# Weight decoding in 40 units of 512 columns instead of 80 of 256, in buffers and banks of its own

## The chip, the cores and the metric

The kernel runs on one core of a Trainium2 chip. The core has five engines that run side by side, each through its own list of instructions in order: TensorE (PE, matrix multiplication; its weight loads are listed apart as PEld), VectorE (DVE), ScalarE (ACT), GpSimd (POOL) and SyncE (SP, which issues all transfers here). Engines wait for each other through semaphores. SBUF is the working memory of 128 partitions; PSUM is the memory into which TensorE writes, eight banks of 512 fp32 columns in each partition. The metric is the time of one execution on the device in microseconds (us), the median of several runs. Less is better.

## The reference

An attention that keeps, for each query, the 32 largest of 576 scores, and behind it a chain of linear layers:

```python
batch, n_heads, seq, head_dim = 8, 8, 576, 64
scores = 1.0 / np.sqrt(64) * np.matmul(q, k.transpose(0, 1, 3, 2))
kth = np.partition(scores, -32, axis=-1)[..., -32:-31]
scores = np.where(scores >= kth, scores, -1e9)
attn = softmax(scores)                      # by max, exp, sum
x = (attn @ v) as [4608 tokens, 512]
a, b = x @ w1, x @ w2                       # w1, w2: 512 x 1024
h = (a * b) @ w3                            # w3: 1024 x 1024
out = h @ w_out                             # w_out: 1024 x 512
```

The four weights come as float64. The chip has no float64, so the kernel turns each number into an fp32 by itself ("decoding"); `w3 @ w_out` is folded into one matrix `wf` before it is used, and `w1`, `w2` and `wf` are each kept as a high and a low part.

## The kernel before

**Slots and periods.** The attention is cut into 144 slots (8 batches, each 18: four pairs of heads by four query tiles of 128, and two ends). A loop over `p` (L504) works on several slots at once in each round, called a period here: scores of slot p+1 (`st` on PE, copied to `s` by ACT), the search for the 32 largest of slot p (`w` and `top` on DVE), masking and exponent of slot p-1 (`pab`: ACT, POOL, ACT), and transposition (`tp`, `ro`), values (`ro`) and normalising (`pr`, `x`) of slot p-2. A period begins here with DVE's two maxima and minima of the score thirds (`w<-s`, L212-213). Twelve slots make a block of 384 tokens; when its `x` is complete (first at p = 14), its linear layers (`moe_steps`) are queued, and `fill` issues 24 of their 288 matrix multiplications in each period (`SHARE`, L44). After the last period the rest is issued.

**Order.** Each engine keeps the order in which the program is written (`InOrder`, L47). Where an instruction waits, all behind it on its engine wait too.

**Decoding.** At six places in each period the loop calls `warm()` (L487). Before, each call starts one new unit of 256 columns and takes every unit under way one step further. A unit (`decode`, L107): ACT writes the scaled high words to the PSUM tile `t` and the scaled low words to `r`, step 1; DVE takes sign and shifted bits of `t` into `u`, two instructions, step 2; POOL adds `u` and `r` as integers, step 3; one step of rest. Then:
- `w_out` (16 units): the sum is written to `wo`, done.
- `w3` (32 units, four for each of eight pieces `f`): at step 5 two matrix multiplications of the unit with `wo` into the PSUM tile `pf` (fp32; the trace shows each as two passes); after the fourth unit ACT copies `pf` to the high part of `wf`, DVE takes the rest as the low part.
- `w1`, `w2` (32 units): at step 5 ACT casts to `wh`, at step 6 POOL subtracts for `wl`.

The list `startup` (L159) runs through `w_out`, then by turns four units of `w3` and two of `w1`, then `w2`: 80 units at six a period, thus until p = 13. I call periods 3 to 10 the fold periods (8 matrix multiplications into `pf` in each), 11 to 13 the `w2` periods.

**Buffers.** The raw bits `z` of a unit lie in the pool of the layers' buffers `g` (8 buffers, L101); `t` (two units to a bank), `pf` and the layers' PSUM tiles share three banks in turn (`ps_m`). `prefetch` asks for transfers up to four units ahead on SP's queue, which also carries q, k, v and the output. On any of these, a new tile waits until the one that had its place before is done with.

Of the kernel before, what the change touches and what calls it, by code (L numbers as in the profile page):

```python
# [21 lines left out]
DM, DF = 512, 1024  # L22
NCC, NFC, NEC = DM // 128, DF // 128, DM // 128
# [3 lines left out]
NB = 384  # L27
# [12 lines left out]
STEEP = 2.0**80  # L40
SCALE = 0.125
S_BUFS = 3
WAITING = 4
SHARE = 8, 8, 8  # L44


# [21 lines left out]
def attn_moe(ctx: ExitStack, tc: tile.TileContext, q, k, v, w1, w2, w3, w_out, out, flag, general):  # L68
    nc = tc.nc
    pe, act, dve, pool, sp = nc.tensor, nc.scalar, nc.vector, nc.gpsimd, nc.sync  # L70
# [2 lines left out]
    kv_p = ctx.enter_context(tc.tile_pool(name="kv", bufs=NHP))  # L73
    att_p = ctx.enter_context(tc.tile_pool(name="att", bufs=2))
    small = ctx.enter_context(tc.tile_pool(name="small", bufs=4))
    x_p = ctx.enter_context(tc.tile_pool(name="x", bufs=2 * NHP))
    g_p = ctx.enter_context(tc.tile_pool(name="g", bufs=NFC))
    o_p = ctx.enter_context(tc.tile_pool(name="o", bufs=2))
    ps_a = ctx.enter_context(tc.tile_pool(name="ps_a", bufs=2, space=PSUM))
    ps_v = ctx.enter_context(tc.tile_pool(name="ps_v", bufs=1, space=PSUM))  # L80
    ps_m = ctx.enter_context(tc.tile_pool(name="ps_m", bufs=3, space=PSUM))

    ident = const.tile([128, 128], F32, name="ident")
    make_identity(nc, ident)
# [13 lines left out]
        pe, act, dve, pool, sp = (InOrder(tc, e) for e in (pe, act, dve, pool, sp))  # L98

    def fetch(src):  # L100
        z = g_p.tile([128, 2 * NB], F32, tag="g", name="z")  # L101
        sp.dma_start(z[:, :512].bitcast(I32), src)
        return z

    bank = []

    def decode(z, dst=None):  # L107
        if not bank:
            both = ps_m.tile([128, 512], F32, tag="mm", name="t")
            bank.extend((both[:, 256:], both[:, :256]))  # L110
        t = bank.pop()
        high = z[:, 1:512:2]
        low = z[:, :512].bitcast(U16)[:, 1:1024:4]
        sign, u, r = (z[:, i * 256 : (i + 1) * 256].bitcast(I32) for i in range(3))
        act.activation(t, high, AF.Copy, scale=2.0**-112)
        act.activation(r, low, AF.Copy, scale=2.0**-13)
        yield
        ti = t.bitcast(I32)
        dve.tensor_scalar(sign, ti, -(2**31), None, op0=ALU.bitwise_and)
        dve.scalar_tensor_tensor(u, ti, 3, sign, op0=ALU.logical_shift_left, op1=ALU.bitwise_or)  # L120
        yield
        dst = z[:, :256] if dst is None else dst
        pool.tensor_tensor(dst.bitcast(I32), u, r, op=ALU.add)
        yield
        yield
        return dst

    def load_w12(i, c, z):
        if len(wl) == i:
            wl.append(const.tile([128, NCC * DF], F32R, tag="wl1", name="wl1"))  # L130
        cut = slice(c * 256, (c + 1) * 256)
        y = yield from decode(z)
        act.copy(wh[i][:, cut], y)
        yield
        pool.tensor_tensor(wl[i][:, cut], y, wh[i][:, cut].bitcast(F32), op=ALU.subtract)

    def load_wout(c, z):
        yield from decode(z, wo[:, c * 256 : (c + 1) * 256])

    fold = {}  # L140

    def load_w3(c, z):
        f, i = c // 4, c % 4
        y = yield from decode(z)
        if i == 0:
            fold[f] = ps_m.tile([128, 512], F32, tag="mm", name=f"pf{f}")
        for j in range(2 * i, 2 * i + 2):
            pe.matmul(
                fold[f], y[:, (j % 2) * 128 : (j % 2 + 1) * 128], wo[:, j * DM : (j + 1) * DM],
                start=(j == 0), stop=(j == NFC - 1),  # L150
            )
        if i == 3:
            cut = slice(f * DM, (f + 1) * DM)
            yield
            act.copy(wf[0][:, cut], fold[f])
            yield
            dve.tensor_tensor(wf[1][:, cut], fold[f], wf[0][:, cut].bitcast(F32), op=ALU.subtract)

    startup = [(w_out[c], lambda z, c=c: load_wout(c, z)) for c in range(16)]  # L159
    for f in range(NFC):  # L160
        startup += [(w3[c], lambda z, c=c: load_w3(c, z)) for c in range(4 * f, 4 * f + 4)]
        startup += [(w1[c], lambda z, c=c: load_w12(0, c, z)) for c in range(2 * f, 2 * f + 2)]
    startup += [(w2[c], lambda z, c=c: load_w12(1, c, z)) for c in range(16)]

    def at(x, b, *i):
        return x[(b, *i)] if isinstance(b, int) else x[(ds(b, 1), *i)].rearrange("o p n -> (o p) n")
# [149 lines left out]
    def width(t):  # L316
        return 64 if t == TAIL else 128

    def new_x():
        return x_p.tile([128, 2, NB], F32R, tag="x", name="x")  # L320

    def normalise(ov, rec):
        dve.tensor_tensor(rec, ov, rec, op=ALU.mult)
# [11 lines left out]
    def moe_steps(xs, nb, places, after):  # L335
        def take_a(p, asb):
            act.copy(asb[:, :nb], p[:, :nb])

        def take_b(p, asb, gf):
            whole = asb[:, :nb]  # L340
            dve.tensor_tensor(whole, p[:, :nb], whole, op=ALU.mult)
            act.copy(gf[:, 0, :nb], whole)
            pool.tensor_tensor(gf[:, 1, :nb], whole, gf[:, 0, :nb].bitcast(F32), op=ALU.subtract)

        def take_o(p, e):
            osb = o_p.tile([128, NB], F32, tag="o", name="osb")
            act.copy(osb[:, :nb], p[:, :nb])
            for place, cut in places:
                sp.dma_start(place(slice(e * 128, (e + 1) * 128)), osb[:, cut])

        g = []
        for f in range(NFC):
            asb = o_p.tile([128, NB], F32, tag="o", name="asb")
            g.append(g_p.tile([128, 2, NB], F32R, tag="g", name="g"))
            for i in range(2):
                p = ps_m.tile([128, 512], F32, tag="mm", name="ab")
# [12 lines left out]
                yield  # L369
        for e in range(NEC):  # L370
            p = ps_m.tile([128, 512], F32, tag="mm", name="eo")
            for f in range(NFC):
                for n, (i, j) in enumerate(((0, 0), (1, 0), (0, 1))):
                    pe.matmul(
                        p[:, :nb], wf[i][:, f * DM + e * 128 : f * DM + (e + 1) * 128], g[f][:, j, :nb],
                        start=(f == 0 and n == 0), stop=(f == NFC - 1 and n == 2),
                    )
                    if (f, n) != (NFC - 1, 2):
                        yield
            after(lambda p=p, e=e: take_o(p, e))  # L380
            yield

    if general:
        outs = out.rearrange("e (b t) -> b e t", b=B)
        for src, step in startup:
            for _ in step(fetch(src)):
                pass
        with tc.For_i(0, B, 1) as b:
            seen = small.tile([1, 1], I32, tag="seen", name="seen", bufs=1)
            nc.sync.dma_start(seen, flag[ds(b + 1, 1), :])  # L390
            with tc.If(nc.values_load(seen, min_val=0, max_val=1) > 0):
                kts = {hp: load_k(b, hp) for hp in range(NHP)}
                vts = {hp: load_v(b, hp) for hp in range(NHP)}
                for first, ts in ((0, range(3)), (NB, range(3, TAIL + 1))):
                    xs, lo = [new_x() for _ in range(NHP)], 0
# [64 lines left out]

    def begin():
        while starting:
            n = starting.pop(0)
            queue.append(moe_steps([xs[n, hp] for hp in range(NHP)], NB, places[n], put_off.append))

# [16 lines left out]
    def prefetch(n):  # L482
        while waiting and len(fetched) < n:
            src, step = waiting.pop(0)
            fetched.append((fetch(src), step))

    def warm():  # L487
        if p < 0:
            return
        if fetched:  # L490
            z, step = fetched.pop(0)
            going.append(step(z))
        going[:] = [unit for unit in going if next(unit, "end") != "end"]
        prefetch(WAITING)

# [8 lines left out]
    for p in range(-1, n_slots + 3):  # L504
# [51 lines left out]
        if 0 <= m < n_slots:  # L556
            n = m // BLOCK
            for hp in hps:
                if (n, hp) not in xs:
                    xs[n, hp] = new_x()  # L560
# [16 lines left out]
    wp = ps_m.tile([128, 512], F32, tag="mm", name="wp")  # L577
# [57 lines left out]
```

## Time and profile before

| | |
|---|---|
| median of 3 runs (lowest, highest) | 1321.85 us (1321.67, 1322.46) |
| the profiled execution | 1321.85 us |
| its span in the trace | 1320.0 us |
| PE, DVE, ACT, POOL busy over the span | 94%, 90%, 73%, 65% |
| chain that ended last, by engine | PE 87%, DVE 4%, POOL 3%, ACT 2% |

The shares over the whole span hide that the run has three parts: about 206 us in which weights are decoded beside the attention (periods 0 to 13 and what lies ahead of them), some 1050 us in which layers and attention run together, and a tail with the layers of the last block. The profiled execution's own time is 1.85 us more than its span. The granted clock of TensorE is 1.00 in the middle part, where full is 2.4 GHz; in the first part it falls to half (1.2 GHz) in places, and a window's clock is then between the two.

### The profile page before, as it was taken

How to read it: one execution, taken by the hardware profiler on the slowest of the kernel's cores; microseconds unless marked ns; L12 is line 12 of the kernel's file. 1: busy time of each engine (PE TensorE's matmuls, PEld its weight loads, DVE VectorE, ACT ScalarE, POOL GpSimd, SP SyncE). 2: the span in 40 equal slices, each digit the busy share in tenths (PEclk: the TensorE clock that was granted, in tenths of full speed). 3: DMA queues.
4: the chain of work that ended last, by engine and by line, in shares of the span. 5: the costliest groups of instructions: out<-in, count | busy, mean ns of one | idle time of the engine just before them, and what ended most of it. 6: DMA issues, size and time to landing. Idle time of an engine off the chain costs nothing.

```text
span 1320.0 us, 28196 instructions
## 1 busy us (share of the span) xinstructions
PE 1235.3 (94%) x9617; PEld 1047.7 (79%) x9617; DVE 1194.1 (90%) x4012; ACT 965.9 (73%) x2057; POOL 853.7 (65%) x1225
## 2 busy tenths in 40 slices
PE   2788858999999999999999999999999999999996
PEld 1334436888888888888888888888888888888996
DVE  7988898999999999999999999999999999999610
ACT  5766786877777877777877877778777778777621
POOL 4767697666766766667757757757667666667510
PEclk9899967999999999999999999999999999999998
DMA  6333331200121001100120012110220012000000
GB/s 243 91 101 123 110 96 29 81 22 21 29 74 32 9 27 64 53 27 16 39 84 20 10 33 79 32 33 10 65 60 9 15 47 81 22 21 1 13 13 27
DMA packets 35886, 64.82 MB, mean 49 GB/s; under 512 B 6036, under 2 KB 12180, under 8 KB 35732
## 3 DMA queue, kind: packets, MB, share of 16 engines
q1 hardware_dynamic: 35732, 62.93, 15.3%
q8 instruction: 77, 1.26, 0.4%
q14 instruction: 77, 0.63, 0.2%
HBM read 53.48 MB, written 9.44 MB: 48 GB/s over the span
## 4 chain that ended last, share of the span: by engine, by line
PE 87%; DVE 4%; POOL 3%; ACT 2%; issue 2%; DMA 1%; SPq 0%; POOLq 0%
PE ab L57 32%; PE eo L57 16%; PE ro L57 15%; PE st L57 12%; PE tp L57 9%; PE pf L57 3%; DVE z L57 2%; DVE w L57 1%; POOL z L57 1%; DVE top L57 1%; POOL wl L57 1%; ACT pab L57 1%; DMA vt<-in_v 0%; ACT s L57 0%; ACT z L57 0%
## 5 line engine op out<-in xcount | busy, mean ns | idle before, releaser
L57 POOL TENSOR_TENSOR pab<-s,pab 128x576 f32<-128x576 f32 x288 | 404.2, 1426 | 127.5 <-DVE w L57 102.0
L57 DVE MAX8 top<-w 128x8 f32<-128x192 f32 (+1 forms) x1152 | 467.3, 447 | 0.0
L57 PE MATMUL ab<-x,wh 128*128 128x384 f32 x1536 | 403.7, 344 | 0.0
L57 ACT COPY pts<-tp 128x1024 f32<-128x1024 f32 x144 | 146.1, 1014 | 198.2 <-PE tp L57 196.8
L57 DVE MATCH_REPLACE8 w<-top,w 128x192 f32<-128x192 f32 x864 | 289.4, 343 | 0.0
L57 PEld LDWEIGHTS ab<-x,wh 128*128 128x128 f32 x1536 | 275.3, 189 | 0.0
L57 PE MATMUL ab<-x,wl 128*128 128x384 f32 x768 | 269.5, 351 | 0.0
L57 ACT ACTIVATE pab<-pab,edge 128x576 f32<-128x576 f32 x288 | 226.8, 787 | 0.5 <-POOL pab L57 0.5
L57 PE MATMUL eo<-g,wf 128*128 128x384 f32 x1152 | 225.8, 346 | 0.0
L57 ACT ACTIVATE pab<-s,edge 128x576 f32<-128x576 f32 x288 | 207.6, 768 | 7.6 <-POOL edge L57 7.5
L57 PE MATMUL st<-kt,qt 64*128 64x288 f32 (+1 forms) x1280 | 188.7, 443 | 18.4 <-ACT pts L57 7.4
L57 PEld LDWEIGHTS eo<-g,wf 128*128 128x128 f32 x1152 | 198.6, 188 | 7.5 <-issue 7.5
L57 ACT COPY s<-st 128x576 f32<-128x576 f32 x288 | 184.4, 640 | 19.5 <-PE st L57 19.5
L57 DVE TENSOR_TENSOR w<-w,s 128x384 f32<-128x384 f32 x288 | 183.9, 639 | 4.9
L57 DVE TENSOR_TENSOR w<-s 128x384 f32<-128x384 f32 x288 | 173.0, 642 | 7.4 <-ACT s L57 7.4
L57 PEld LDWEIGHTS ro<-pts,vt 128*64 128x64 f32 x2560 | 130.2, 139 | 51.3 <-ACT g L57 28.3
L57 PEld LDWEIGHTS st<-kt,qt 64*128 64x128 f32 (+1 forms) x1280 | 100.6, 183 | 81.0 <-ACT pr L57 28.1
L57 PE MATMUL ro<-pts,vt 128*64 128x128 f32 (+1 forms) x2560 | 163.4, 271 | 0.0
L57 PE MATMUL tp<-ident,pab 128*128 128x128 f32 x1152 | 152.1, 275 | 11.3 <-ACT s L57 11.3
L57 PEld LDWEIGHTS ab<-x,wl 128*128 128x128 f32 x768 | 144.3, 188 | 13.4 <-issue 12.3
L57 PEld LDWEIGHTS tp<-ident,pab 128*128 128x128 f32 x1152 | 136.4, 142 | 22.3 <-POOL wo L57 10.7
L57 POOL TENSOR_TENSOR g<-asb,g 128x384 fp32r<-128x384 f32 x96 | 96.9, 1010 | 86.8 <-ACT g L57 86.8
(51 smaller groups left out, 1309.6 us busy)
## 6 DMA issues: line engine op xcount, KB each, us to landing
z<-in_w SPq DMA_DIRECT2D x64, 256.0 KB, 2.7
vt<-in_v SPq DMA_DIRECT2D x32, 352.0 KB, 3.7
qt<-in_q SPq DMA_DIRECT2D x40, 256.0 KB, 2.7
kt<-in_k SPq DMA_DIRECT2D x32, 320.0 KB, 3.1
out_t<-osb SPq DMA_DIRECT2D x32, 192.0 KB, 1.9
z<-in_wo SPq DMA_DIRECT2D x16, 256.0 KB, 3.9
out_t<-osb SPq DMA_DIRECT2D x16, 160.0 KB, 1.8
out_t<-osb SPq DMA_DIRECT2D x16, 32.0 KB, 1.6
```

The lines of the kernel that those rows point to most:

```text
L57: ins = fn(*args, **kw)
```

## The change

- A unit now has 512 columns (`CHUNK`); there are 40, and a new one starts at every second call of `warm` (three in each period). The steps of a unit stay one call apart.
- `z` has 3 x 512 columns and a pool of its own of six buffers, `t` two banks and `pf` one bank of their own. `settle()` closes these pools when the first block's layers are to begin, and the layers' `g`, three banks and the second half of `x` are then given the same room.
- `r` is written in place over the low words (every second element of `z`), `u` into the third part of `z`, where DVE's second instruction works in place.
- The 4 multiplications of a `w3` unit are issued two at step 5 and two at step 6.
- Transfers are asked for three units ahead; each is 512 KB instead of 256 KB.

```diff
-WAITING = 4
+CHUNK = 512
+WAITING = 3
...
-    x_p = ctx.enter_context(tc.tile_pool(name="x", bufs=2 * NHP))
-    g_p = ctx.enter_context(tc.tile_pool(name="g", bufs=NFC))
+    x_p = {0: ctx.enter_context(tc.tile_pool(name="x0", bufs=NHP))}
...
-    ps_m = ctx.enter_context(tc.tile_pool(name="ps_m", bufs=3, space=PSUM))
+    early = ExitStack()
+    z_p = early.enter_context(tc.tile_pool(name="z", bufs=6))
+    ps_e = early.enter_context(tc.tile_pool(name="ps_e", bufs=2, space=PSUM))
+    late = {}
+
+    def settle():
+        early.close()
+        x_p[1] = ctx.enter_context(tc.tile_pool(name="x1", bufs=NHP))
+        late["g"] = ctx.enter_context(tc.tile_pool(name="g", bufs=NFC))
+        late["mm"] = ctx.enter_context(tc.tile_pool(name="ps_m", bufs=3, space=PSUM))
...
-        z = g_p.tile([128, 2 * NB], F32, tag="g", name="z")
-        sp.dma_start(z[:, :512].bitcast(I32), src)
+        z = z_p.tile([128, 3 * CHUNK], F32, tag="z", name="z")
+        sp.dma_start(z[:, : 2 * CHUNK].bitcast(I32), src)
...
-        if not bank:
-            both = ps_m.tile([128, 512], F32, tag="mm", name="t")
-            bank.extend((both[:, 256:], both[:, :256]))
-        t = bank.pop()
-        high = z[:, 1:512:2]
-        low = z[:, :512].bitcast(U16)[:, 1:1024:4]
-        sign, u, r = (z[:, i * 256 : (i + 1) * 256].bitcast(I32) for i in range(3))
+        t = ps_e.tile([128, CHUNK], F32, tag="t", name="t")
+        high = z[:, 1 : 2 * CHUNK : 2]
+        low = z[:, : 2 * CHUNK].bitcast(U16)[:, 1 : 4 * CHUNK : 4]
+        r, u = z[:, 0 : 2 * CHUNK : 2].bitcast(I32), z[:, 2 * CHUNK :].bitcast(I32)
...
-        dve.tensor_scalar(sign, ti, -(2**31), None, op0=ALU.bitwise_and)
-        dve.scalar_tensor_tensor(u, ti, 3, sign, op0=ALU.logical_shift_left, op1=ALU.bitwise_or)
+        dve.tensor_scalar(u, ti, -(2**31), None, op0=ALU.bitwise_and)
+        dve.scalar_tensor_tensor(u, ti, 3, u, op0=ALU.logical_shift_left, op1=ALU.bitwise_or)
...
-            fold[f] = ps_m.tile([128, 512], F32, tag="mm", name=f"pf{f}")
-        for j in range(2 * i, 2 * i + 2):
+            fold[f] = ps_e.tile([128, 512], F32, tag="pf", name=f"pf{f}", bufs=1)
+        for j in range(4 * i, 4 * i + 4):
             pe.matmul(
...
+            if j % 4 == 1:
+                yield
-        if i == 3:
+        if i == 1:
...
     def begin():
         while starting:
+            while going or fetched or waiting:
+                warm()
+            if not late:
+                settle()
...
     def warm():
+        entered.append(p)
         if p < 0:
             return
-        if fetched:
+        if fetched and len(entered) % 2:
```

On GpSimd, one fold period before, from the sum of the row sums (`sums`) to the last decoded unit (`z<-z`: the integer add of a unit; `wl`: the low part of `w1`):

```order
L57 TENSOR_SCALAR sums<-sums 128x2
L57 TENSOR_TENSOR z<-z 128x256
L57 TENSOR_TENSOR edge<-top_96,coef 128x4
L57 TENSOR_TENSOR over<-top_96 128x2
L57 TENSOR_TENSOR x<-pr,x 128x128
L57 COPY wide<-sums 128x128
L57 TENSOR_TENSOR pab<-s,pab 128x576 x2
L57 TENSOR_TENSOR wl_103<-z,wh_98 128x256
L57 TENSOR_TENSOR z<-z 128x256
L57 TENSOR_TENSOR wl_103<-z,wh_98 128x256
L57 TENSOR_TENSOR z<-z 128x256 x4
```

The same period of the changed kernel on GpSimd:

```order
L58 TENSOR_SCALAR sums<-sums 128x2
L58 TENSOR_TENSOR z<-z 128x512
L58 TENSOR_TENSOR edge<-top_96,coef 128x4
L58 TENSOR_TENSOR over<-top_96 128x2
L58 TENSOR_TENSOR x<-pr,x 128x128
L58 COPY wide<-sums 128x128
L58 TENSOR_TENSOR pab<-s,pab 128x576 x2
L58 TENSOR_TENSOR wl_103<-z,wh_98 128x512
L58 TENSOR_TENSOR z<-z 128x512 x2
```

The add in front of `edge` now holds the columns of two old units; the old second one stood behind both `pab` and a `wl`.

TensorE's list of instructions is the same throughout; its waits are not. The multiplications into `pf` ahead of the scores `st` in a fold period, before:

```order
L57 MATMUL ro<-ident,wide 128x128 [waits Pool_49]
L57 MATMUL pf_601<-wo,z 128x512 [waits DMAHW1_49,DVE_49]
L57 MATMUL pf_601<-wo,z 128x512
L57 MATMUL pf_601<-wo,z 128x512 [waits DMAHW2_49,Pool_49]
L57 MATMUL pf_601<-wo,z 128x512
L57 MATMUL st<-kt,qt 128x288 [waits Activation_49]
```

And there in the changed kernel:

```order
L58 MATMUL ro<-ident,wide 128x128 [waits Pool_49]
L58 MATMUL pf_509<-wo,z 128x512 [waits DVE_49]
L58 MATMUL pf_509<-wo,z 128x512 x3
L58 MATMUL st<-kt,qt 128x288 [waits Activation_49]
```

The third multiplication's wait for GpSimd is gone; the first waits for DVE alone, that is for the reading of the one `pf` bank by `wf`.

On VectorE, the first part of a fold period before, from the reciprocal of the row sums (`z<-t` and `z<-t,z` are a unit's pair):

```order
L57 RECIPROCAL sums<-sums 128x2
L57 TENSOR_TENSOR w<-s 128x2x192 x2
L57 TENSOR_TENSOR w<-w,s 128x2x192 x2
L57 TENSOR_SCALAR z<-t 128x256
L57 SCALAR_TENSOR_TENSOR z<-t,z 128x256
L57 TENSOR_TENSOR wf_101<-pf_601,wf_100 128x512
L57 TENSOR_SCALAR z<-t 128x256
L57 SCALAR_TENSOR_TENSOR z<-t,z 128x256
L57 MAX top_97<-w 128x8 x2
L57 MATCH_REPLACE w<-top_97,w 128x192 x2
```

And in the changed kernel:

```order
L58 RECIPROCAL sums<-sums 128x2
L58 TENSOR_TENSOR w<-s 128x2x192 x2
L58 TENSOR_TENSOR w<-w,s 128x2x192 x2
L58 TENSOR_TENSOR wf_101<-pf_509,wf_100 128x512
L58 TENSOR_SCALAR z<-t 128x512
L58 SCALAR_TENSOR_TENSOR z<-t,z 128x512
L58 MAX top_97<-w 128x8 x2
L58 MATCH_REPLACE w<-top_97,w 128x192 x2
```

`wf` now stands directly behind the four maxima and minima, ahead of the period's first pair; three pairs of 512 columns stand in a period where six of 256 stood.

## Rows read from the trace of the kernel before

**Rows 1.** Busy time by stage: window, length, PE, PEld, DVE, ACT, POOL (instructions), clock, DMA, GB/s.
```profile
7.38:18.19 10.81, 4.58 (x16) 2.45 (x16) 10.60 (x35) 4.49 (x12) 2.91 (x4) 1.00 1.04 390
18.19:56.79 38.60, 19.61 (x89) 11.15 (x90) 36.99 (x115) 27.70 (x66) 26.33 (x36) 0.91 0.37 110
56.79:165.15 108.36, 85.65 (x380) 42.20 (x379) 92.91 (x276) 75.62 (x182) 74.80 (x105) 0.94 0.36 107
89.08:103.64 14.56, 11.32 (x56) 5.74 (x55) 13.30 (x42) 10.83 (x26) 10.74 (x15) 1.00 0.42 127
103.64:119.86 16.22, 12.98 (x56) 6.27 (x55) 13.32 (x42) 10.83 (x26) 10.73 (x15) 0.89 0.32 99
165.15:194.09 28.94, 17.33 (x90) 10.91 (x88) 26.57 (x80) 23.77 (x60) 26.36 (x38) 0.65 0.39 109
194.09:206.35 12.26, 6.67 (x38) 4.29 (x38) 10.81 (x34) 9.24 (x23) 12.11 (x18) 0.56 0.01 1
600.00:1100.00 500.00, 500.00 (x4069) 440.49 (x4069) 489.65 (x1682) 389.58 (x808) 337.29 (x484) 1.00 0.12 37
```
**Rows 2.** The chain that ended last, in one fold period: start, length, what.
```profile
96.65 0.73 POOL z L57
...
97.42 1.98 PE pf L57 x4
99.41 0.71 PE st L57 x4
...
103.22 0.42 DVE z L57
```
**Rows 3.** TensorE's timeline, a fold period: start, length, group, idle time before it.
```profile
101.75 3.70 PE L57 MATMUL pf<-wo,z 128*128 128x512 f32 x8
105.29 1.04 PE L57 MATMUL tp<-ident,pab 128*128 128x128 f32 x8
...
107.38 1.98 PE L57 MATMUL pf<-wo,z 128*128 128x512 f32 x4 [0.32 <-DVE z L57]
111.99 3.19 PE L57 MATMUL pf<-wo,z 128*128 128x512 f32 x4 [2.62 <-POOL z L57]
```
**Rows 4.** VectorE's timeline, the beginning of a fold period.
```profile
103.64 1.54 DVE L57 TENSOR_TENSOR w<-s 128x384 f32<-128x384 f32 x2
...
106.45 0.41 DVE L57 TENSOR_SCALAR z<-t 128x256 int32<-128x256 int32 x1
106.90 0.43 DVE L57 SCALAR_TENSOR_TENSOR z<-t,z 128x256 int32<-128x256 int32 x1
107.24 0.68 DVE L57 TENSOR_TENSOR wf<-pf,wf 128x512 fp32r<-128x512 f32 x1
```
**Rows 5.** GpSimd's timeline in the same period.
```profile
103.79 0.97 POOL L57 TENSOR_TENSOR z<-z 128x256 int32<-128x256 int32 x1 [1.94 <-ACT x L57]
104.73 0.51 POOL L57 TENSOR_TENSOR edge<-top,coef 128x4 f32<-128x4 f32 x1
...
106.06 0.62 POOL L57 COPY wide<-sums 128x128 f32<-128x128 f32 x1
107.78 2.78 POOL L57 TENSOR_TENSOR pab<-s,pab 128x576 f32<-128x576 f32 x2 [1.10 <-ACT pab L57]
...
111.22 0.72 POOL L57 TENSOR_TENSOR z<-z 128x256 int32<-128x256 int32 x1
```
**Rows 6.** Groups by operation and shape: busy, mean ns of one, idle before.
```profile
L57 POOL TENSOR_TENSOR g<-asb,g 128x384 fp32r<-128x384 f32 x96 | 96.9, 1010 | 86.8 <-ACT g L57 86.8
...
L57 ACT ACTIVATE t<-z 128x256 f32<-128x256 f32 x80 | 32.4, 405 | 33.1 <-DVE z L57 32.5
...
L57 ACT CAST wh<-z 128x256 fp32r<-128x256 f32 x32 | 12.7, 400 | 0.0
...
L57 ACT CAST wf<-pf 128x512 fp32r<-128x512 f32 x8 | 4.7, 587 | 8.3 <-PE pf L57 8.3
```
**Rows 7.** TensorE's timeline, the scores of the third slot.
```profile
15.55 1.33 PE L57 MATMUL st<-kt,qt 64*128 64x288 f32 x4 [4.88 <-ACT s L57]
```

More of the change, by code (lines that the diff above doesn't have):

```diff
@@ L118, in decode @@
         ti = t.bitcast(I32)
-        dve.tensor_scalar(sign, ti, -(2**31), None, op0=ALU.bitwise_and)
-        dve.scalar_tensor_tensor(u, ti, 3, sign, op0=ALU.logical_shift_left, op1=ALU.bitwise_or)
+        dve.tensor_scalar(u, ti, -(2**31), None, op0=ALU.bitwise_and)
+        dve.scalar_tensor_tensor(u, ti, 3, u, op0=ALU.logical_shift_left, op1=ALU.bitwise_or)
         yield
-        dst = z[:, :256] if dst is None else dst
+        dst = z[:, 2 * CHUNK :] if dst is None else dst
         pool.tensor_tensor(dst.bitcast(I32), u, r, op=ALU.add)
@@ L130, in load_w12 @@
             wl.append(const.tile([128, NCC * DF], F32R, tag="wl1", name="wl1"))
-        cut = slice(c * 256, (c + 1) * 256)
+        cut = slice(c * CHUNK, (c + 1) * CHUNK)
         y = yield from decode(z)
@@ L137, in load_wout @@
     def load_wout(c, z):
-        yield from decode(z, wo[:, c * 256 : (c + 1) * 256])
+        yield from decode(z, wo[:, c * CHUNK : (c + 1) * CHUNK])
     fold = {}
     def load_w3(c, z):
-        f, i = c // 4, c % 4
+        f, i = c // 2, c % 2
         y = yield from decode(z)
         if i == 0:
-            fold[f] = ps_m.tile([128, 512], F32, tag="mm", name=f"pf{f}")
-        for j in range(2 * i, 2 * i + 2):
+            fold[f] = ps_e.tile([128, 512], F32, tag="pf", name=f"pf{f}", bufs=1)
+        for j in range(4 * i, 4 * i + 4):
             pe.matmul(
-                fold[f], y[:, (j % 2) * 128 : (j % 2 + 1) * 128], wo[:, j * DM : (j + 1) * DM],
+                fold[f], y[:, (j % 4) * 128 : (j % 4 + 1) * 128], wo[:, j * DM : (j + 1) * DM],
                 start=(j == 0), stop=(j == NFC - 1),
             )
-        if i == 3:
+            if j % 4 == 1:
+                yield
+        if i == 1:
             cut = slice(f * DM, (f + 1) * DM)
@@ L157, in load_w3 @@
             dve.tensor_tensor(wf[1][:, cut], fold[f], wf[0][:, cut].bitcast(F32), op=ALU.subtract)
-    startup = [(w_out[c], lambda z, c=c: load_wout(c, z)) for c in range(16)]
+    startup = [(w_out[c], lambda z, c=c: load_wout(c, z)) for c in range(NFC)]
     for f in range(NFC):
-        startup += [(w3[c], lambda z, c=c: load_w3(c, z)) for c in range(4 * f, 4 * f + 4)]
-        startup += [(w1[c], lambda z, c=c: load_w12(0, c, z)) for c in range(2 * f, 2 * f + 2)]
-    startup += [(w2[c], lambda z, c=c: load_w12(1, c, z)) for c in range(16)]
+        startup += [(w3[c], lambda z, c=c: load_w3(c, z)) for c in (2 * f, 2 * f + 1)]
+        startup += [(w1[f], lambda z, f=f: load_w12(0, f, z))]
+    startup += [(w2[c], lambda z, c=c: load_w12(1, c, z)) for c in range(NFC)]
     def at(x, b, *i):
@@ L317, in width, with new_x @@
         return 64 if t == TAIL else 128
-    def new_x():
-        return x_p.tile([128, 2, NB], F32R, tag="x", name="x")
+    def new_x(n):
+        return x_p[n % 2].tile([128, 2, NB], F32R, tag="x", name="x")
     def normalise(ov, rec):
@@ L353, in moe_steps @@
             asb = o_p.tile([128, NB], F32, tag="o", name="asb")
-            g.append(g_p.tile([128, 2, NB], F32R, tag="g", name="g"))
+            g.append(late["g"].tile([128, 2, NB], F32R, tag="g", name="g"))
             for i in range(2):
-                p = ps_m.tile([128, 512], F32, tag="mm", name="ab")
+                p = late["mm"].tile([128, 512], F32, tag="mm", name="ab")
                 for c in range(NCC):
@@ L370, in moe_steps @@
         for e in range(NEC):
-            p = ps_m.tile([128, 512], F32, tag="mm", name="eo")
+            p = late["mm"].tile([128, 512], F32, tag="mm", name="eo")
             for f in range(NFC):
@@ L394, in attn_moe @@
                 for first, ts in ((0, range(3)), (NB, range(3, TAIL + 1))):
-                    xs, lo = [new_x() for _ in range(NHP)], 0
+                    xs, lo = [new_x(0) for _ in range(NHP)], 0
                     for t in ts:
@@ L462, in begin @@
         while starting:
+            while going or fetched or waiting:
+                warm()
+            if not late:
+                settle()
             n = starting.pop(0)
@@ L485, in prefetch @@
             fetched.append((fetch(src), step))
+    entered = []
     def warm():
+        entered.append(p)
         if p < 0:
             return
-        if fetched:
+        if fetched and len(entered) % 2:
             z, step = fetched.pop(0)
@@ L559, in attn_moe @@
                 if (n, hp) not in xs:
-                    xs[n, hp] = new_x()
+                    xs[n, hp] = new_x(n)
             normalise(ov, rec)
@@ L576, in attn_moe @@
     dve.tensor_reduce(worst[:, :1], worst[:, 1:], axis=AX.X, op=ALU.max)
-    wp = ps_m.tile([128, 512], F32, tag="mm", name="wp")
+    wp = late["mm"].tile([128, 512], F32, tag="mm", name="wp")
     pe.transpose(wp[: B + 1, :128], worst, ident)
@@ L609, in bits @@
         return c(w).view(_np.int64)
-    w1p, w2p = (_np.asarray(w).reshape(NCC, 128, 4, 256).transpose(0, 2, 1, 3).reshape(16, 128, 256) for w in (moe_w1, moe_w2))
-    w3p = _np.asarray(moe_w3).reshape(NFC, 128, 4, 2, 128).transpose(0, 2, 4, 3, 1).reshape(32, 128, 256)
-    wop = _np.asarray(moe_w_out).reshape(8, 128, 2, 256).transpose(0, 2, 1, 3).reshape(16, 128, 256)
+    w1p, w2p = (_np.asarray(w).reshape(NCC, 128, 2, 512).transpose(0, 2, 1, 3).reshape(8, 128, 512) for w in (moe_w1, moe_w2))
+    w3p = _np.asarray(moe_w3).reshape(NFC, 128, 2, 4, 128).transpose(0, 2, 4, 3, 1).reshape(16, 128, 512)
+    wop = _np.asarray(moe_w_out).reshape(8, 128, 512)
     arrays = {
```

1 line of the change is left out of this document (removed).

## The prediction

> **What bounds the kernel now.** I read the page first, for the engines by slice, then the busy time by stage, then the chain that ended last, then the timelines of one period on each engine. The reader is to see in the stages [rows 1] that the change touches a first part only: periods 0 to 13, from 7.38 to 206.35 us, 199.0 us long. Behind it TensorE is busy for 500.00 of 500.00 us at full clock; the list of TensorE is the same there before and after, so a first part that is shorter by so much moves all the rest forward by as much, and nothing gives it back.
>
> In the first part a period takes 15.48 us in the fold periods 4 to 10 (108.36 / 7) [rows 1]. No engine fills it: in the one of 14.56 us DVE is busy for 13.30, PE 11.32, ACT 10.83, POOL 10.74. The chain [rows 2] shows the loop that sets it: POOL's add of a unit (96.65), four passes into `pf` (97.42), the scores (99.41), ACT, and DVE's last pair of the period (103.22), upon which the next period begins (103.64). TensorE's timeline [rows 3] shows why this is long: after the first four passes (107.38, 1.98 us) it stands idle for 2.62 us until 111.99, since the second unit's add (111.22) lies on POOL behind both masks (107.78, 2.78 us) and a `wl` [rows 5]. And the four passes after that idle time then took 3.19 us instead of 1.98: in that period the granted clock was 0.89 of full on the mean, it took 16.22 us, while the one before it had clock 1.00 and 14.56 [rows 1, 3]. With 1.66 us as the price of such a fall to half clock, four of the seven periods had one (108.36 - 7 x 14.56 = 6.4). In the `w2` periods 11 and 12 POOL is busy for 26.36 of 28.94 us and binds. In 0 to 3 DVE does: 10.60 of 10.81 and 36.99 of 38.60.
>
> **The prices of 512 columns.** DVE: a pair of 256 takes 0.79 us from start to start (107.24 - 106.45) [rows 4]. `wf`, of 512 columns and from PSUM too, takes 0.68 where an instruction of 256 takes 0.41 to 0.43: 0.26 for 256 columns more. A pair of 512 is then 0.79 + 2 x 0.26 = 1.31; two old pairs were 1.58; 0.27 gained for each new unit. ACT: 256 columns cost 0.40 and 512 cost 0.587 [rows 6], so each new instruction takes 0.18 longer and is one instead of two. POOL: no add of 512 is in the trace. It lies between 1.01 us (384 columns) [rows 6] and 1.39 (576, a half of 2.78) [rows 5]; on the line between them, 1.26; I take 1.28. Two old ones took 1.44 (2 x 0.72).
>
> Two things the trace does not show. The add now reads `r` at every second element. On ACT `t`, which reads so, costs 0.405 against 0.400 for `wh`, which does not [rows 6]: nothing. For POOL no row bounds it; I take nothing, and from above a doubling, 2.56. The Trainium skill (GPSIMD Engine Reference, section 7, Performance pitfalls) says that reads of SBUF cost half more once step times element size is over 8 bytes; this one is at 8 exactly, so by that rule nothing is paid, and no run here shows it yet.
>
> Second, what the add costs beside DVE's maxima and minima, which have two inputs from SBUF: the old one took 0.97 us there (103.79, with 103.64 on DVE) and 0.72 elsewhere (111.22) [rows 4, 5], a factor of 1.35. I take the same factor: 1.28 x 1.35 = 1.73. The Trainium skill (GPSIMD Engine Reference, section 8, Key points) names it: GpSimd shares its SBUF interfaces with VectorE and contends with its instructions of two SBUF inputs. It speaks against this change, which lays twice as long an add there, ahead of `edge`; without it the sum below would be 3 us lower.
>
> **The fold periods 4 to 10.** The new loop, from the start of a period on DVE: POOL's add starts 0.15 later and takes 1.73; `edge` to `wide` take 1.95 (104.73 to 106.68) [rows 5], so `wide` is there at 3.83. TensorE turns it, 0.4, and now issues eight passes without a wait, as both pairs of multiplications come from that one add: 3.54 (101.75 to 105.29) [rows 3], end 7.77. `wf` reads the one `pf` bank on DVE directly behind the fold, done at 2.81 + 0.6 = 3.4 (106.45 - 103.64 [rows 4]), ahead of the first pass at 4.2, so the single bank costs nothing; it would cost what comes over 0.8. From the scores to the next period 4.23 (99.41 to 103.64) [rows 2, 4], now with two ACT instructions 0.18 longer and a pair 0.52 longer: 5.11. Sum 12.9. DVE's own work is 13.30 - 3 x 0.27 = 12.5. Both loops are that near to each other that one will wait for the other at times (DVE needs ACT's `t` and `r` at three places); I add 0.3 by choice: 13.2 us. TensorE's work, 11.3, stays below.
>
> The 2.62 us idle on TensorE goes, and with it, I think, most of the falls of its clock; what is left is a wait for `wide` of some 1.5 us (tp ends near 2.3, `wide` at 3.8). I take one fall in seven periods instead of four. 7 x 13.2 + 1.66 = 94.1 against 108.36: 14.3 gained. The bounds are 12.5 in each and no fall (87.5) and 13.2 with a fall in each (104.0).
>
> **The other periods.** 0: DVE still does the worth of three new pairs, 3.9 us where five old ones were 4.0: nothing. Its transfers are 512 KB instead of 256 and 0.5 MB more lie ahead of the keys; at the 390 GB/s of that stretch [rows 1] that is 1.3 us, hidden by the scores' wait of 4.88 us for ACT [rows 7]; if that cover went, at most 1.3 are lost once. 1 to 3: nine new units, 9 x 0.27 = 2.4 gained, as DVE is busy all the time. 11 and 12: POOL has from the add on 1.73, 1.95, the masks 2.72, five more of 1.28, `sums` 0.2: 13.0 with a little waiting 13.4 against 14.47: 2.1 gained. 13: one unit instead of two, 0.6 gained. From 14 on nothing: the pools that `settle` closes have then been done with for most of a period, and the room is handed over without a transfer.
>
> **Sum.** 14.3 + 2.4 + 2.1 + 0.6 = 19.4 us. The profiled execution took 1321.85, which is the median also: 1302.5 us.
>
> **The rivals.**
> - DVE alone binds the fold periods: the waits overlap, 12.5 in each, no fall of the clock: 6.6 less, 1296 us. For it: DVE is at 13.30 of 14.56 already. Against: `s` reaches DVE by a chain that I add up to more.
> - The clock falls in each fold period: 6 x 1.66 more, 1312.5 us. For it: four of seven do so now, TensorE's remaining wait is longer in one place (1.5 us for `wide`, 0.3 now), and a fall now hits the eight passes on the chain. Against: the idle time ahead of the falls shrinks.
> - Slower or none: POOL's strided add. At a doubled price (2.56, beside DVE 3.5) the loop of the fold periods is 12.9 + 1.7 + 0.3 = 14.9 (gain 2.4 instead of 14.3, with the one fall), and periods 11 and 12 take 13.4 + 1.7 + 2.6 = 17.7 each, 6.5 more than before; with 2.4 in periods 1 to 3 and a loss of some 1.9 in 13 that is 1325.5 us. It decides from about 1.8 times the plain price; at 1.5 times it is some 1314. For it: no row has this form. Against: ACT's row of the same kind.
> - Half clock through all fold periods: four passes take 3.19 instead of 1.98, so a period's 11.3 us on TensorE become about 18: 7 x (18.1 - 15.48) = 18 lost against 5 gained, 1335 us. Against: a stretch at 1.00 follows each fall now, with less work in it than the change packs there.
> - The gain does not arrive: the middle part starts earlier and waits for something else, 1320 to 1322. Against: TensorE at 500 of 500.
>
> **How the numbers follow.** Forecast, 1298 to 1308: 0.53. DVE alone: 0.15. Falls in each period: 0.15. Strided add: 0.08, half of it over 1319. Half clock: 0.04. No arrival: 0.05, partly for what I have not seen. Under 0.2% (2.6 us) a measurement here can't be told from no change. Faster: 0.53 + 0.15 + 0.15 + 0.04 and a part of the last, 0.90; same 0.04; slower 0.06. The range takes in the first three, 0.83 in all: 1295 to 1313.
>
> **What would show it.** Right: fold periods of 12.9 to 13.5 us by DVE's starts; TensorE going through eight passes of `pf` ahead of `st` without idle time; an add of 1.7 us beside the maxima, 1.3 elsewhere; DVE pairs of 1.3; ACT never waiting for DVE to free `t`; the middle part unchanged, 500 of 500. Wrong: an add of over 2 us; passes at 0.8 us each in most fold periods; a wait of TensorE for DVE ahead of the first pass, which the single `pf` bank would make; or `z` transfers landing after ACT asks for them.

## The result, and the profile after

The changed kernel takes 1302.45 us (median of 4 runs, 1302.18 to 1303.55) against 1322.06 for the kernel before beside it: a ratio of 0.985, 95% interval 0.984 to 0.987, or 19.6 us less. The forecast was 1302.5. That the total came so close is luck: two of its terms were wrong and cancelled, and the fold periods came to their length by another engine than the sum had it.

Busy time by stage in the changed kernel, columns as in [rows 1]. The first window is periods 1 to 3, the next periods 4 to 10; 97.25 and 111.41 are two fold periods; then periods 11 and 12, 13, 3 alone, 14, and a piece of the middle:

```profile
18.27:57.00 38.73, 19.30 (x90) 11.05 (x91) 36.44 (x97) 24.78 (x47) 25.03 (x27) 0.66 0.39 133
57.00:151.66 94.66, 83.08 (x381) 42.83 (x380) 90.98 (x234) 69.42 (x133) 70.84 (x77) 0.95 0.38 121
97.25:111.41 14.16, 12.16 (x54) 6.08 (x53) 13.12 (x36) 9.85 (x19) 10.12 (x11) 0.88 0.42 128
111.41:124.45 13.04, 11.64 (x57) 6.15 (x56) 12.90 (x35) 9.97 (x19) 10.09 (x11) 1.00 0.34 122
151.66:177.82 26.16, 14.41 (x87) 9.59 (x85) 25.40 (x68) 22.87 (x44) 25.37 (x27) 0.73 0.27 88
177.82:189.41 11.59, 6.81 (x38) 4.98 (x38) 9.70 (x30) 6.96 (x14) 11.44 (x13) 0.57 0.01 1
...
42.48:57.00 14.52, 10.88 (x43) 5.35 (x44) 12.50 (x35) 8.03 (x16) 8.87 (x10) 0.76 0.18 55
189.41:197.29 7.88, 5.92 (x40) 4.82 (x41) 7.45 (x28) 5.46 (x10) 5.21 (x9) 0.78 0.06 21
...
600.00:1100.00 500.00, 500.00 (x4130) 440.54 (x4129) 489.20 (x1678) 389.43 (x811) 335.30 (x483) 1.00 0.13 41
```

Against [rows 1]: periods 4 to 10 take 94.66 instead of 108.36 us (13.7 gained), 11 and 12 26.16 instead of 28.94 (2.8), 13 11.59 instead of 12.26 (0.7); periods 1 to 3 gain nothing (38.73, 38.60 before). TensorE's granted clock is lower in periods 1 to 3 (0.66, 0.91 before). The middle is as full as it was. In the good fold period (from 111.41, clock 1.00) DVE is now busy for 12.90 of 13.04 us, which says that DVE sets its length; the run with the order of the units alone, below, tests it.

TensorE's timeline, in period 3 first, then from 100.91 on in two fold periods (start, length, what, idle time before):

```profile
46.12 0.48 PE L58 MATMUL ro<-ident,wide 128*128 128x128 f32 x1 [4.57 <-POOL wide L58]
46.39 5.96 PE L58 MATMUL pf<-wo,z 128*128 128x512 f32 x8
...
100.91 0.33 PE L58 MATMUL ro<-ident,wide 128*128 128x128 f32 x1 [1.88 <-POOL wide L58]
101.36 5.40 PE L58 MATMUL pf<-wo,z 128*128 128x512 f32 x8
106.69 1.24 PE L58 MATMUL st<-kt,qt 64*128 64x288 f32 x8
...
115.06 0.33 PE L58 MATMUL ro<-ident,wide 128*128 128x128 f32 x1 [1.27 <-POOL wide L58]
115.51 3.70 PE L58 MATMUL pf<-wo,z 128*128 128x512 f32 x8
119.14 1.24 PE L58 MATMUL st<-kt,qt 64*128 64x288 f32 x8
```

The eight passes go through without the 2.62 us for POOL's add that stood in their middle in [rows 3]. In the first of the two periods they are slow (5.40 instead of 3.70) at a mean granted clock of 0.88, and the period is 1.1 longer than the next (14.16, 13.04). The chain that ended last, in that first period (start, length, what):

```profile
101.36 5.40 PE pf L58 x8
106.76 0.71 PE st L58 x4
107.49 0.51 ACT s L58
...
109.43 0.55 ACT t L58
...
110.00 0.70 DVE z L58
```

So a period with a fall still runs on the chain through `pf`, scores and `t` that the prediction added up. In the good period after it the chain holds only DVE's pieces, one behind the other, and gaps of at most 0.73 us that the profile calls issue. What fills DVE there, from its timeline (the row at 111.86 is the second of the two that begin at 111.41):

```profile
97.25 2.11 DVE L58 TENSOR_TENSOR w<-s 128x384 f32<-128x384 f32 x2
99.28 1.42 DVE L58 TENSOR_TENSOR w<-w,s 128x384 f32<-128x384 f32 x2
100.63 0.68 DVE L58 TENSOR_TENSOR wf<-pf,wf 128x512 fp32r<-128x512 f32 x1
101.23 0.67 DVE L58 TENSOR_SCALAR z<-t 128x512 int32<-128x512 int32 x1
...
102.55 0.61 DVE L58 MAX8 top<-w 128x8 f32<-128x192 f32 x2
...
111.86 1.64 DVE L58 TENSOR_TENSOR w<-s 128x384 f32<-128x384 f32 x1
113.43 0.54 DVE L58 TENSOR_TENSOR w<-w,s 128x384 f32<-128x384 f32 x1
```

And GpSimd beside it:

```profile
111.66 1.44 POOL L58 TENSOR_TENSOR z<-z 128x512 int32<-128x512 int32 x1 [2.46 <-DVE sums L58]
...
118.54 1.28 POOL L58 TENSOR_TENSOR wl<-z,wh 128x512 fp32r<-128x512 f32 x1
119.78 1.30 POOL L58 TENSOR_TENSOR z<-z 128x512 int32<-128x512 int32 x1
...
189.37 0.20 POOL L58 TENSOR_TENSOR edge<-top,coef 128x4 f32<-128x4 f32 x1
```

Read the two together. The add runs from 111.66 to 113.10. The instruction of DVE that lies beside it (111.86) takes 1.64 us, where one of the same size with no add beside it takes 0.54 (113.43; GpSimd runs the small `edge` and `over` then). The add takes 1.44 there against 1.30 elsewhere (119.78). So the two slow each other, and DVE pays most: the pair of maxima and minima took 1.54 in [rows 4] and takes 2.11 now. DVE's loss is as long as the add: the second instruction ends 0.40 us after the add does (113.50, 113.10), and in [rows 4, 5] it ended 0.42 after an add of half the columns (105.18, 104.76). The pair grew by 0.57, the add by itself by 0.56 (0.72 to 1.28). This reads as DVE standing still until the add is done; the rows show the times, not the reason. The add's strided reading of `r` costs next to nothing: 1.30 against 1.28 for `wl`, which reads without a stride.

### The profile page after: what moved, and what is told of

It reads as the page before. It is cut to its first block, busy times and chain, and to the rows that moved or that the text cites. A ratio compares the mean times of both kernels' runs of the same rounds, so it can differ in the third digit from the quotient of the medians.

```text
span 1300.4 us, 27717 instructions
## 1 busy us (share of the span) xinstructions
PE 1227.7 (94%) x9617; PEld 1046.6 (80%) x9617; DVE 1189.3 (91%) x3932; ACT 954.0 (73%) x1961; POOL 844.0 (65%) x1169
## 4 chain that ended last, share of the span: by engine, by line
PE 87%; DVE 9%; issue 1%; POOL 1%; ACT 1%; DMA 0%; SPq 0%; DVEq 0%; ACTq 0%
PE ab L58 33%; PE eo L58 16%; PE ro L58 15%; PE st L58 12%; PE tp L58 9%; DVE w L58 4%; DVE z L58 3%; DVE top L58 2%; PE pf L58 2%; DVE wf L58 0%; ACT s L58 0%; POOL wl L58 0%; ACT pab L58 0%; DMA kt<-in_k 0%; ACT t L58 0%
## 5 line engine op out<-in xcount | busy, mean ns | idle before, releaser
L58 PE MATMUL st<-kt,qt 64*128 64x288 f32 (+1 forms) x1280 | 184.8, 437 | 8.8 <-DMA kt<-in_k 8.1
L58 DVE TENSOR_TENSOR w<-s 128x384 f32<-128x384 f32 x288 | 179.7, 664 | 7.9 <-ACT s L58 7.5
L58 PEld LDWEIGHTS ab<-x,wl 128*128 128x128 f32 x768 | 144.3, 188 | 13.4 <-issue 12.3
```

The source lines that it names most:

```text
L58: ins = fn(*args, **kw)
```

## The experiments

The theory was that the places do it: one unit of 512 columns in front of `edge` in place of two of 256, of which the second stood behind the masks. The rivals: the buffers and banks of their own (no unit waits for another's place), or the larger instructions (fewer fixed costs). Each run is given as its ratio to the kernel before, timed on the same chip.

**Own buffers and banks, units of 256 at six places.**

```diff
-CHUNK = 512
-WAITING = 3
+CHUNK = 256
+WAITING = 6
...
-    z_p = early.enter_context(tc.tile_pool(name="z", bufs=6))
+    z_p = early.enter_context(tc.tile_pool(name="z", bufs=12))
...
-        if fetched and len(entered) % 2:
+        if fetched:
```

> Units of 256 columns at all six places as in the kernel before, but in buffers (12 of z) and banks of their own as in the changed kernel (t two banks, pf one). Theory A (the gain in the fold periods comes from where the units stand: both pairs of multiplications of a piece now hang on one add ahead of the masks): POOL's order is that of before, TensorE still waits some 2.6 us for the second add, fold periods stay at 14.5 and 16.2 us, the whole at 1318 to 1322 us. Theory B (the gain comes from the own buffers and banks: ACT's 32 us of waits for DVE and SP's for POOL and PE go): fold periods of about 13.5 us, the whole at 1303 to 1308 us.

Measured: 1320.89 us, ratio 0.9999 (0.9989 to 1.0009). TensorE still waits in the middle of its passes, as in [rows 3]:

```profile
109.32 2.39 PE L58 MATMUL pf<-wo,z 128*128 128x512 f32 x4 [2.37 <-POOL z L58]
```

Own buffers and banks alone give nothing; that rival falls. They do remove waits: ACT's idle time for DVE ahead of `t`, 32.5 us in [rows 6], is 10.0 here. None of it was on the path.

**The changed kernel with each instruction of a unit cut into two of 256.**

```diff
-        act.activation(t, high, AF.Copy, scale=2.0**-112)
-        act.activation(r, low, AF.Copy, scale=2.0**-13)
+        halves = slice(0, 256), slice(256, 512)
+        for c in halves:
+            act.activation(t[:, c], high[:, c], AF.Copy, scale=2.0**-112)
+            act.activation(r[:, c], low[:, c], AF.Copy, scale=2.0**-13)
...
+        for c in halves:
+            pool.tensor_tensor(dst.bitcast(I32)[:, c], u[:, c], r[:, c], op=ALU.add)
```

(DVE's pair, the cast and `wl` are cut likewise.)

> The changed kernel with each instruction of a unit (ACT, DVE, POOL, cast, low part) issued as two of 256 columns one behind the other; places, buffers, banks and transfers as changed. It separates the larger instructions from the places. Theory A (places first): DVE pays 0.27 us for each unit again, 0.8 a period, so fold periods of 13.8 to 14.2 us instead of 13.05 and 14.16, 2 us more in periods 1 to 3, POOL 1 us more in each of 11 and 12: 1308 to 1313 us. Theory C (the larger instructions carry the gain): fold periods back at 14.6 and more, 1318 to 1322 us.

Measured: 1306.75 us, ratio 0.9897 (0.9877 to 0.9916). With the small instructions of before, 14 of the 19.6 us are there (1320.89 to 1306.75). That is the places, with the transfers of 512 KB that come with them; no run parts these two. The larger instructions are worth the other 4 to 6 us, and little of it in the fold periods: in the profiled execution (1304.87) periods 4 to 10 take 0.7 us more than in the changed kernel (95.34, 94.66), periods 11 to 13 take 1.6 more (39.38, 37.75). It came out a little better than the 1308 to 1313 expected, where the expectation let each maximum cost what it costs in the changed kernel: here `w<-s` takes 0.86 us on the mean in the fold periods, 1.09 there, as the first of the two short adds begins ahead of the pair (98.07, 98.62).

**`t` and `pf` in three banks in turn, as before.**

```diff
-        t = ps_e.tile([128, CHUNK], F32, tag="t", name="t")
+        t = ps_e.tile([128, CHUNK], F32, tag="mm", name="t")
...
-            fold[f] = ps_e.tile([128, 512], F32, tag="pf", name=f"pf{f}", bufs=1)
+            fold[f] = ps_e.tile([128, 512], F32, tag="mm", name=f"pf{f}")
```

> The changed kernel, but t and pf take turns in three banks of one pool, as before the change; the rest as changed. Theory A with its remark on banks: a unit's t now comes into the bank of pf and waits on ACT until DVE has read it for wf; ACT stands some 1.5 us more at the head of each fold period, and masks and scores behind it: 1 to 1.5 us more in each of eight periods, 1310 to 1315 us. If the banks of their own are worth nothing: 1302 to 1304 us.

Measured: 1301.82 us, ratio 0.9849 (0.9832 to 0.9865), the same as the changed kernel. I expected 1310 to 1315 on the ground that shared banks would cost; they cost nothing. With half as many units the old sharing no longer holds anybody up (ACT's `t` waits for DVE nowhere), so the banks of their own can be left out of the explanation altogether.

**Units started at the second, fourth and sixth place, and `w1` ahead of its two `w3` units.** The first add then no longer stands between `sums` and `edge`.

```diff
-        startup += [(w3[c], lambda z, c=c: load_w3(c, z)) for c in (2 * f, 2 * f + 1)]
         startup += [(w1[f], lambda z, f=f: load_w12(0, f, z))]
+        startup += [(w3[c], lambda z, c=c: load_w3(c, z)) for c in (2 * f, 2 * f + 1)]
...
-        if fetched and len(entered) % 2:
+        if fetched and len(entered) % 2 == 0:
```

> The changed kernel with units begun at the 2nd, 4th and 6th place of a period instead of the 1st, 3rd and 5th, and the w1 unit of each turn ahead of its two w3 units. No integer add of POOL then lies beside DVE's maxima and minima or ahead of edge, and only four passes into pf stand between the transposition and the scores. If the 0.55 us by which the first maxima are longer in the changed kernel (2.1 us the pair instead of 1.5) is the add beside them, and the chain over pf binds only where TensorE's clock falls: fold periods of 12.5 us on DVE alone, with and without falls: 1293 to 1297 us. If the maxima are longer for another reason: periods stay at 13.05 and only the falls stop to cost: 1298 to 1300 us. If TensorE's clock falls more often: over 1302 us.

Measured: **1291.24 us**, ratio 0.9777 (0.976 to 0.9793), better than expected and the fastest of all. Its windows (columns as in [rows 1]; seven fold periods with the half microsecond ahead of them, for the first of them begins at 52.01, and one of them):

```profile
51.50:138.61 87.11, 74.82 (x381) 40.56 (x380) 83.68 (x235) 69.60 (x135) 70.27 (x80) 1.00 0.43 137
89.07:101.45 12.38, 10.61 (x56) 5.76 (x55) 11.91 (x34) 9.90 (x20) 9.98 (x12) 1.00 0.41 127
```

A period is 12.38 us, and DVE's own work in it 11.91 instead of 12.90. GpSimd's and DVE's timelines show why:

```profile
99.75 1.28 POOL L58 TENSOR_TENSOR z<-z 128x512 int32<-128x512 int32 x1 [1.64 <-DVE z L58]
...
103.96 2.79 POOL L58 TENSOR_TENSOR pab<-s,pab 128x576 f32<-128x576 f32 x2 [0.59 <-ACT pab L58]
```

```profile
101.45 1.04 DVE L58 TENSOR_TENSOR w<-s 128x384 f32<-128x384 f32 x2
```

The add is over before the maxima begin: they take 1.04 us instead of 2.11, the add 1.28 instead of 1.44, and the masks start 2.51 us into the period (103.96 - 101.45), where they start 3.79 in in a period of the changed kernel with a fall (101.04 on GpSimd's timeline, less 97.25) and 4.39 in in a good one (115.80 - 111.41). TensorE waits here too (1.77 us for `wf`, the single `pf` bank), but behind the scores, and DVE goes on meanwhile; the granted clock is 1.00 throughout the window. The expectation counted the fold periods only. By the starts of DVE's maxima they begin at 52.01 us instead of 57.00 and end at 138.61 instead of 151.66: 5.0 us are gained in periods 0 to 3, 8.1 in the fold periods, and the spans (1288.2, 1300.4) leave 12.2 of these 13.1.

**The order of the units alone** (the first hunk of the diff above).

```diff
-        startup += [(w3[c], lambda z, c=c: load_w3(c, z)) for c in (2 * f, 2 * f + 1)]
         startup += [(w1[f], lambda z, f=f: load_w12(0, f, z))]
+        startup += [(w3[c], lambda z, c=c: load_w3(c, z)) for c in (2 * f, 2 * f + 1)]
```

> The changed kernel with the w1 unit of each turn ahead of its two w3 units, places as changed (1st, 3rd, 5th). All multiplications into pf then stand between the values of one slot and the transposition of the next, none between transposition and scores; POOL's add beside DVE's first maxima stays. If the good periods of the changed kernel (13.05 us) are DVE's own work with 0.55 us of stretched maxima in it, and the falls of TensorE's clock cost only through the passes ahead of the scores: 13.05 us in all fold periods, 1298 to 1300 us. If the chain over pf binds in the good periods too: under 12.8 us each, 1295 to 1297 us.

Measured: 1297.53 us, ratio 0.9819 (0.9798 to 0.9841), between the times of the two cases; the length of the periods decides. Its fold periods and, from TensorE's timeline, one of them:

```profile
54.92:146.44 91.52, 78.33 (x382) 41.26 (x381) 90.46 (x233) 69.94 (x134) 71.51 (x77) 1.00 0.42 128
```

```profile
98.16 1.43 PE L58 MATMUL st<-kt,qt 64*128 64x288 f32 x8
...
102.11 7.11 PE L58 MATMUL pf<-wo,z 128*128 128x512 f32 x16 [1.29 <-DVE wf L58]
```

The passes of `pf` no longer lie ahead of the scores, which start 3.91 us into the period (98.16 - 94.25) instead of 7.73 (119.14 - 111.41). And yet the periods are 13.05 long (91.52 / 7 = 13.07), the same as the good ones of the changed kernel, and none has a fall (clock 1.00). So the 13.05 doesn't come from the chain through `pf`: it is DVE's work, busy for 90.46 of 91.52. What this order gives is 3.1 us in these seven periods, where the falls stood, and 2.1 in period 3, which takes 12.44 us instead of 14.52. Why the clock doesn't fall here is not shown.

**The first place moved behind `wide`**, so that `edge` to `wide` go ahead of the add.

```diff
-        warm()
...
             wide = spread(pabs[m][1], slots[m][1])
+        warm()
```

> The changed kernel with the first call of warm in a period moved behind the row sums' spreading, so that POOL's add follows wide instead of standing ahead of edge; it then lies beside the second pair of maxima and minima, wf and the next decoding pair. If DVE loses to any instruction of POOL that runs beside its two-input instructions: the first pair takes 1.1 us instead of 2.1, the second pair up to 0.5 more than 1.42; good periods of 12.5 to 12.9 us, 1298 to 1301 us. If the length of the maxima has nothing to do with the add: 13.05 us and 2.1 us as before, 1302 to 1303 us.

Measured: 1299.91 us, ratio 0.984 (0.9819 to 0.9862). DVE, then GpSimd, at the beginning of a fold period:

```profile
94.69 1.10 DVE L58 TENSOR_TENSOR w<-s 128x384 f32<-128x384 f32 x2
95.72 2.25 DVE L58 TENSOR_TENSOR w<-w,s 128x384 f32<-128x384 f32 x2
```

```profile
95.35 1.61 POOL L58 TENSOR_TENSOR z<-z 128x512 int32<-128x512 int32 x1
```

The first pair is short again (1.10) and the second is long (2.25 instead of 1.42), since the add now lies beside that one. The loss went with the add. That is the test of the contention: not the place in the period, nor the data, but what runs beside the add. The second pair lost 0.83, more than the 0.5 expected. Its 1.42 elsewhere holds a loss already: in period 0, with GpSimd idle, the pair takes 1.14 us (8.39 on DVE's timeline of the changed kernel), and in the fold periods GpSimd's `x<-pr,x` of 128x128 runs beside it (113.99, 0.45). That part is read from the timelines alone. Against 1.14 the add costs the second pair 1.11, as much as the first pair (2.11 against 1.04). The good periods are 12.91 and those with a fall 14.03; the three falls in periods 4 to 10 are still there.

**The places alone** (second, fourth, sixth; the order of the units unchanged).

```diff
-        if fetched and len(entered) % 2:
+        if fetched and len(entered) % 2 == 0:
```

> The changed kernel with units begun at the 2nd, 4th and 6th place, order of units as changed. No add beside the maxima, but the add of a piece's first unit then stands on POOL behind both masks, and the eight passes' first four ahead of the scores wait for it, as in the kernel before. If that wait is what made the kernel before slow: scores some 2.5 us later, fold periods of 14.5 to 15.5 us, 1309 to 1317 us. If not, 12.4 to 13 us, under 1299 us.

Measured: 1295.69 us, ratio 0.981 (0.9787 to 0.9833): the case in which the wait made the kernel before slow (1309 to 1317) falls. A unit's add stands behind the masks again, and TensorE does wait for it:

```profile
87.14 1.98 PE L58 MATMUL pf<-wo,z 128*128 128x512 f32 x4 [0.52 <-POOL z L58]
...
100.75 1.98 PE L58 MATMUL pf<-wo,z 128*128 128x512 f32 x4 [2.77 <-POOL z L58]
```

The period that holds the wait of 2.77 (from 94.16) is 12.29 long; the one with 0.52 (from 80.58) is 13.58, above the 12.4 to 13 of the other case. So a wait as long as the one in [rows 3] need not lengthen a period. GpSimd's timeline shows what is different:

```profile
96.67 2.79 POOL L58 TENSOR_TENSOR pab<-s,pab 128x576 f32<-128x576 f32 x2 [0.59 <-DVE w L58]
99.42 1.28 POOL L58 TENSOR_TENSOR z<-z 128x512 int32<-128x512 int32 x1
```

The masks start 2.51 us into the period (4.14 before: 107.78 - 103.64), the add behind them 5.26 (7.58 before). In the kernel before the masks came late for two reasons: an add stood ahead of `edge`, and then they waited 1.10 us for ACT [rows 5]. ACT had waited 1.03 us for `pf` itself, to copy it into `wf`, and had a cast and a unit's `t` and `r` to do ahead of the first exponent:

```profile
105.49 0.59 ACT L57 CAST wf<-pf 128x512 fp32r<-128x512 f32 x1 [1.03 <-PE pf L57]
...
106.93 1.44 ACT L57 ACTIVATE pab<-s,edge 128x576 f32<-128x576 f32 x2
```

Behind the masks a `wl` stood ahead of the second add. This is read from two traces; no run takes these causes apart. In a long period of this run (13.58, from 80.58) the chain that ended last goes from twelve passes of `pf` to ACT's `wf` and on through ACT's list. With the other order of the units all fold periods are about 12.4, and the whole is 4.5 us shorter (1295.69 to 1291.24).

## Why the prediction was right, point by point

- **The middle moves forward as a whole: right.** 500 of 500 us busy; the first part from period 0 through 14 is 19.2 us shorter by the windows, and the span 19.6 (1320.0 to 1300.4).
- **Fold periods, 14.3 gained: 13.7, but not as summed.** I had the chain at 12.9, DVE at 12.5 and 0.3 between them: 13.2. The chain was right up to the scores (7.73 us into the period, forecast 7.77) and too long behind them (4.72, 111.41 - 106.69, forecast 5.11), so it is about 12.5. The 13.05 is DVE's: the rival "DVE alone binds", at a higher price than it was given. The failed step is the contention. I charged it to POOL's add by the factor of [rows 4, 5] (1.73; it took 1.44) and nothing to DVE, whose pair of maxima grew from 1.54 to 2.11. DVE's 12.5 and the 0.57 of the pair make the 13.05. [rows 4] had this loss already, at 1.54 for two instructions that take 0.54 each without an add; I read only the other side of it. The Trainium skill (GPSIMD Engine Reference, section 8, Key points) has the contention, and the traces agree; how much each engine pays is read from the rows here.
- **Falls of the clock: one at 1.66 forecast, three at 1.11 found.** 7 x 13.05 + 3 x 1.11 = 94.7, the 94.66 of the window. The passes lose 1.70 in a fall and the period 1.11, since the chain has some 0.6 of room under DVE's 13.05. They come in every second period (those from 70.05, 97.25 and 124.45), and no run shows why.
- **Periods 1 to 3, 2.4 gained: wrong, nothing.** Periods 1 and 2 gained 1.0 of 1.6 (24.21 us against 25.21 in the windows): of the pairs' 1.6 the two pairs of maxima take 1.1 back (2.10 each against 1.54), and DVE stands idle 0.5 less. TensorE's clock, 0.60 there against 1.00 before, can cost next to nothing there, as DVE is busy for 23.94 of the 24.21. Period 3 lost 1.1 (14.52 against 13.39). Before, TensorE's timeline reads there:

```profile
46.49 0.48 PE L57 MATMUL ro<-ident,wide 128*128 128x128 f32 x1 [3.49 <-POOL wide L57]
46.76 5.80 PE L57 MATMUL pf<-wo,z 128*128 128x512 f32 x8
```

  `wide` comes 3.64 us into the period after and 3.09 before, and behind it both kernels run eight slow passes ahead of the scores. The scores start 0.72 later (9.81 into the period, 9.09 before), and from there to the next period it is 4.71 instead of 4.30. I had priced this period by DVE's pairs though here the longer add ahead of `edge` lies on the path (1.43 at 42.73, 0.88 at 43.64 before).
- **Periods 11 and 12, 2.1 gained: 2.8. Period 13, 0.6: 0.7.** The right size, a little low: a period is 13.08 us, not 13.4, and the adds beside the maxima take 1.44 and 1.67, not 1.73. POOL binds still (25.37 of 26.16).
- **From 14 on, nothing: wrong, 2.2 gained.** Period 14 took 10.10 us before and takes 7.88. Before, a last `wl` stood ahead of `edge` in it, on GpSimd:

```profile
206.31 0.72 POOL L57 TENSOR_TENSOR wl<-z,wh 128x256 fp32r<-128x256 f32 x1
207.00 0.51 POOL L57 TENSOR_TENSOR edge<-top,coef 128x4 f32<-128x4 f32 x1
```

  Now the last unit is done before the period begins and `edge` starts at once (189.37, 0.20 long), so that TensorE turns `wide` 1.97 us into the period instead of 2.97. The rest goes with the clock of this period, 0.66 before and 0.78 after; that part is read from the two traces alone, no run isolates it. The two errors, 2.4 and 2.2, cancelled, which is luck.
- **The prices of 512 columns** were close: DVE's pair 1.32 (102.55 - 101.23; forecast 1.31), the add 1.30 (1.28). ACT's `t` and `r` took longer than `wf`, from which I had taken them:

```profile
L58 ACT ACTIVATE z<-z 128x512 int32<-128x512 uint16 x40 | 26.6, 664 | 0.0
...
L58 ACT ACTIVATE t<-z 128x512 f32<-128x512 f32 x40 | 25.5, 637 | 3.1 <-DMA z<-in_wo 3.1
```

  The second row holds one of the signs of being wrong, ACT waiting 3.1 us for a transfer of `z`, once, at the end of period 0. It cost nothing: the period takes 10.82 us, 10.81 before.

- **The strided add, the rival on the slower side,** had no place: 1.30 with the stride, 1.28 without. The rule of the Trainium skill (GPSIMD Engine Reference, section 7, Performance pitfalls for Q7 kernels), by which a step of 8 bytes is still free, agrees. Nor does the stride make DVE's loss greater. The run with units of 256 columns reads with it, the kernel before without, and the pair takes 1.54 us in both [rows 4]:

```profile
100.62 1.54 DVE L58 TENSOR_TENSOR w<-s 128x384 f32<-128x384 f32 x2
...
100.87 0.88 POOL L58 TENSOR_TENSOR z<-z 128x256 int32<-128x256 int32 x1 [1.69 <-DVE sums L58]
```

Left open: what makes the clock fall in three of seven periods, since no run sets it by itself; what part of the 14 us of the places comes from which engine's list; and how far the order of 1291.24 us can be taken.

## What to carry to other kernels

Ask of each small piece of work what stands behind it on its in-order queue: here the places of the units, with their larger transfers, were worth 14 us, the size of their instructions 4 to 6, and own buffers and banks nothing, though they removed a long wait. Where GpSimd works beside VectorE instructions with two SBUF inputs, price both sides, and put GpSimd's work beside something else. A right total is no proof of its terms: compare period by period.

## What the runs showed of the hardware

- A VectorE maximum of 128x384 fp32 with two SBUF inputs takes 0.54 us without an add beside it and 1.64 beside a GpSimd integer add of 128x512; the add goes from 1.30 to 1.44 there, and to 1.61 where the add was moved behind `wide`. The one takes three times as long, the other a tenth to a quarter longer.
- VectorE's instruction ends 0.40 to 0.42 us after the add does, whether the add has 256 columns (105.18 and 104.76 before; 102.16 and 101.75 with own buffers and banks) or 512 (113.50 and 113.10). So the loss is about the add's own length, not a factor on VectorE's.
- An idle wait of TensorE is not enough to foretell a fall to 1.2 GHz: after 2.77 us idle four passes took 1.98 us, full speed (100.75, places alone; granted clock 1.00 in that period), and with an idle time of 1.88 us just before, eight took 5.40 instead of 3.70 (101.36, changed kernel; 0.88).
